# Ranking all eight experts by token count: the first two places are picked early, behind chunks 6 and 7

## The chip, the cores and the metric

One NeuronCore of a Trainium2 chip runs the whole program. The metric is the device time of one execution in microseconds (us), lower is better.

## What is computed

Three stages on 2304 tokens of width 512: local plus downsampled attention, a gated MLP, and a mixture of 8 experts with one expert per token. The last stage is the one the change works on:

```python
logits = xn @ en.T / tau
expert_idx = np.argmax(logits, axis=1)
...
for e in range(E):
    mask = expert_idx == e
    h = np.maximum(x[mask] @ w1[e], 0.0)
    out[mask] = gate_w[mask, None] * (h @ w2[e])
```

`w1[e]` is 512 x 1024 and `w2[e]` 1024 x 512, in f32. The inputs are fixed (seed 0). Counted with the reference, the experts get 297, 284, 329, 305, 296, 231, 280 and 282 tokens.

## The kernel before

**Work and order.** The tokens go through the gated MLP in 9 chunks of 256 (chunks 2 and 3, and 4 and 5, as pairs). Behind each chunk its rows are stored to `x2d` in DRAM, the router picks an expert per token, and `base`, a running count per expert (plus the start of that expert's part of the table), is raised. The tokens' entries (row, gate) go by an indirect DMA, a scatter, into two tables `tab` in DRAM. Then the experts run one after another in eight *places*. A place has a fixed number of columns (`CAPS`, line 50): token slots that are computed whether they are filled or not. Every product is made of three matmuls, with each operand split into a high and a low part.

**A place.** For a place the kernel reads its table rows (`tb`, line 1699 for places 0 and 1; 1760 and 1766 for the others), merges the two tables on DVE (line 1705), gathers the tokens' rows from `x2d` into `xs` (line 1720; in groups of 32 rows, line 1792, from place 2 on), transposes them on TensorE (line 1731), splits them, and runs layer 1 (line 1851, the place's columns as the moving operand) and layer 2 (line 1957 with the columns moving for places 1 to 6; line 1861 with 512 moving columns for places 0 and 7 and for the last 80 slots of place 0). That is 96 matmuls of line 1851 and 96 of line 1957 for a place from 1 to 6. Weights come in eight loads of 512 KB (lines 1663 and 1666, on the SP queue), each cast to a high part on ACT (line 1644) and subtracted on DVE (line 1647): a *split* is the pair.

**Which expert sits where.** Place 0 is always expert 0 (`FIXED = 1`), so its weights and its first 256 slots can be fetched while chunk 8 still runs. The other seven are ranked by count behind chunk 8 (`last_base`, line 1415): rank by comparing all pairs, then the inverse permutation into `ordi` (line 1435). SP and POOL load `ordi` into registers (line 1460), and every address of places 1 to 7 is computed from them. A queue that loads a register waits there for DVE's `ordi`; what stands behind it in that queue waits too. Place 1 has the same 336 columns as place 0, the others 312, 304, 288, 288, 288 and 256. If a count is over its place's columns, a block at the end (line 2168) computes the rest.

**What sets the order.** A planner written into the kernel (`Sched`) runs all steps as generators with planned durations, priorities and buffer slots, and so fixes in advance the order of instructions on each engine and queue; the hardware keeps that order and waits by semaphores. A weight load takes three slots of the pool `w`: one for the raw weights, two for the parts; slots come back from the gated MLP's weights as chunk 8 finishes with them. The DMA itself only waits for its raw slot.

Of the kernel before, what the change touches and what calls it, by code (L numbers as in the profile page):

```python
# [11 lines left out]
F32 = mybir.dt.float32  # L12
# [3 lines left out]
I32 = mybir.dt.int32  # L16
# [3 lines left out]
ALU = mybir.AluOpType  # L20
AX = mybir.AxisListType
# [3 lines left out]
P = 128  # L25
# [5 lines left out]
E = 8  # L31
# [8 lines left out]
NCHUNK = NTOK // CT  # L40
# [5 lines left out]
CAP = sum(SLT)  # L46
NSL = len(SLT)
EARLY = 256
FIXED = 1
CAPS = (CAP, CAP, 312, 304, 288, 288, 288, 256)  # L50
SLTE = [tuple(m for m in (P, P, n - 2 * P) if m) for n in CAPS]
NOV = -(-(NTOK - EARLY) // P)
EST = EARLY + NOV * P
FREE = float(np.uint32(0x3FFFFFFF).view(np.float32))
NEG = -1.0e30
NT18 = NTOK // P
NRK = E - FIXED
NCST = P + P // 2 + NPAIR * WK // 2 + 3 * E + 4 * NT18 + NOV + NRK
NEYE = P + P // 2
DMA_T = 700.0  # L60
# [233 lines left out]
def build(tc, a):  # L294
    nc = tc.nc
# [11 lines left out]
    out = a["out"]  # L307
# [3 lines left out]
    sc = Sched()  # L311
# [6 lines left out]
    def op(eng, ns, prio=None, how=None):  # L318
        return ("op", eng, ns, prio, how)
# [29 lines left out]
    o = 0  # L349
# [25 lines left out]
    rk = cst.tile([P, 4, NRK], F32, name="rk")  # L375
    rk2 = cst.tile([P, NRK, NRK], F32, name="rk2")
    ordi = cst.tile([P, NRK], I32, name="ordi")
    nc.gpsimd.memset(cape, float(CAP))


    slots("w", wp, NW, [P, 1024], True)
# [1033 lines left out]
    def last_base():  # L1415
        yield op("DVE", 75, -0.9, True)
        nc.vector.tensor_tensor(out=base, in0=base, in1=base0, op=ALU.subtract)
        r0, lo = iota8[:, 0, 0:NRK], iota8[:, 0, FIXED:]
        key, rank, val = rk[:, 0], rk[:, 1], rk[:, 2]
        inner = lambda x: x.unsqueeze(1).to_broadcast([P, NRK, NRK])  # L1420
        outer = lambda x: x.unsqueeze(2).to_broadcast([P, NRK, NRK])
        yield op("DVE", 75, -0.9, True)
        nc.vector.scalar_tensor_tensor(out=key, in0=lo, scalar=-1.0 / 16, in1=base[:, FIXED:], op0=ALU.mult, op1=ALU.add)
# [18 lines left out]
        nc.vector.tensor_reduce(out=cape[:, FIXED:], in_=rk2, axis=AX.X, op=ALU.add)  # L1442
# [11 lines left out]
    def set_order():  # L1454

        yield ("wait", "order")
        yield ("lag", 500)
        for i in range(NRK):
            on_ = [mybir.EngineType.SP] + ([mybir.EngineType.Pool] if FIXED + i == 1 else [])
            turn[FIXED + i] = nc.values_load(ordi[0:1, i:i + 1], engines=on_, min_val=FIXED, max_val=E - 1,  # L1460
                                             skip_runtime_bounds_check_because="a permutation of the ranked experts")
        sc.set("turns")

    def expert_of(x, e):

        return x[e] if e < FIXED else x[bass.ds(turn[e], 1)].rearrange("o r c -> (o r) c")

    def tab_rows(t, e, lo, hi):
        return expert_of(tabs[t].rearrange("(e s) w -> e s w", e=E)[:, lo:hi, :], e)
# [126 lines left out]
    def route_base(c, lp, rp):  # L1596
        for m in range(2):
            yield op("DVE", 80, -0.9)
            nc.vector.tensor_tensor(out=base, in0=base, in1=rp[:, 1, m, :], op=ALU.add)
        sc.put("ps", lp)  # L1600
        if c == NCHUNK - 2:

            yield op("DVE", 75, -0.9)
            nc.vector.tensor_scalar(out=base[:, 0:1], in0=base[:, 0:1], scalar1=float(EARLY), scalar2=None, op0=ALU.max)
        sc.set(("base", c))

    def store_x2(c, m, row):
        t = 2 * c + m
# [42 lines left out]
    def load_experts():  # L1651
        yield ("wait", ("g1", NCHUNK - 2))
        for e in range(E):
            if e == FIXED:
                yield ("wait", "turns")
            for nm, dst in (("w1", w1s), ("w2", w2s)):
                for i in range(4):
                    lo = yield ("get", "w")
                    hi = yield ("get", "w")
                    raw = yield ("get", "w")  # L1660
                    yield dma(P * 4096)
                    if nm == "w1":
# [11 lines left out]
    def load_slots(e, parts):  # L1674

        if e not in xss:
            xh = yield ("get", "xh")
            xl = yield ("get", "xl")
            tb = ep[0].tile([P, 2, NSL, 4], I32, tag=f"tb{e % 3}", name=f"tb{e}")
            xss[e] = (xh, xl, tb[:, 0])  # L1680
            tbs[e] = tb
        xh, xl = xss[e][0:2]
        tb = tbs[e]
        xhr, xlr = xh.bitcast(F32R), xl.bitcast(F32R)
        first = [j for j in parts if (e, j) in ((0, 2), (1, 0))]
        for j in first:
            sc.spawn(sc.cur.prio + 0.1 * j, load_slot(e, j, tb[:, 0], xhr, xlr))
        if (e, 2) == (0, parts[0]) or e == 1:
            for m in range(2):
                yield ("wait", ("tab", NCHUNK - 1) if m else "tab0")  # L1690
        soon = e == 0 or e == 1
        js = slice(parts[0], parts[-1] + 1)
        if e >= FIXED:
            yield ("wait", "turns")
        for t in range(2):
            yield op("POOL", 700, -1.0) if soon else dma(P * 48)
            if t == 0:
                sc.cur.t -= sc.LAT["POOL"] if soon else sc.LAT_DMA
            (nc.gpsimd if soon else nc.sync).dma_start(
                out=tb[:, t, js], in_=tab_rows(t, e, js.start * P, js.stop * P).rearrange("(j p) w -> p j w", p=P))  # L1700
        if soon:
            yield ("lag", 2900)
            yield tick()
        yield op("DVE", 80, -1.0, True)
        nc.vector.tensor_tensor(out=tb[:, 0, js], in0=tb[:, 0, js], in1=tb[:, 1, js], op=ALU.bitwise_and)
        tb = tb[:, 0]
        for j in parts:
            sc.set(("tb", e, j))
            if j not in first:
                sc.spawn(sc.cur.prio + 0.1 * j, load_slot(e, j, tb, xhr, xlr))  # L1710
# [424 lines left out]
    with tc.manual_schedule():  # L2135
# [93 lines left out]
def consts():  # L2229
# [8 lines left out]
    for n in range(NT18):  # L2238
# [3 lines left out]
    one = m.transpose(1, 2, 0, 3).reshape(64, NU * WK)  # L2242
    parts = [np.eye(P, dtype=np.float32), halves(np.eye(P, dtype=np.float32)), halves(m.reshape(P, -1)), np.tile(e, (P, 2)), np.tile(EST * e, (P, 1)),
             t.reshape(P, -1).view(np.float32), np.tile(EARLY + P * np.arange(NOV, dtype=np.float32), (P, 1)),
             np.tile(np.array(CAPS[FIXED:], np.float32), (P, 1))]
# [43 lines left out]
```

## Time and profile before

| | us |
|---|---|
| median of 3 runs (all three) | 811.74 (811.62, 811.74, 813.75) |
| the profiled execution, its own time | 808.81 |
| its span, first to last instruction | 807.2 |
| TensorE busy | 789.4 (98%), clock 0.997 of full speed |
| DVE, ACT, POOL busy | 563.2, 369.1, 195.1 |

Times in the trace count from the start of the span. Chunk 8's first matmul starts at 514.7, place 0's at 567.2, place 1's at 603.5, place 2's at 635.6, and the span ends at 807.2. Busy TensorE time overlaps (matmuls are pipelined), so how fast it goes is read from starts.

### The profile page before, as it was taken

The page shows a single profiled execution, that of the slowest core. Times are in us where ns is not written, and L with a number is a line of the kernel's source. Part 1 is how long each engine was busy: PE and PEld are TensorE (multiplying, and loading weights), DVE is VectorE, ACT ScalarE, POOL GpSimd, SP SyncE. Part 2 cuts the span into 40 slices and gives each one's busy share as a digit, 9 for nine tenths or more (in the row PEclk, how much of TensorE's full clock was granted, in tenths as well). Part 3 has the DMA queues.
Part 4 walks back from the last instruction along what each step waited for, and adds up shares of the span by engine and source line. Part 5 has one row for each costly group of instructions (what it writes and reads, how often), then busy time and mean ns, then how long its engine had stood idle before and what let it go on. Part 6 is the DMA issues. An engine that isn't in the chain of part 4 may idle for free. (4 is left out here: it accounts for less than half of the span.)

```text
span 807.2 us, 16215 instructions
## 1 busy us (share of the span) xinstructions
PE 789.4 (98%) x6122; PEld 691.1 (86%) x6128; DVE 563.2 (70%) x1472; ACT 369.1 (46%) x919; POOL 195.1 (24%) x208
## 2 busy tenths in 40 slices
PE   8989999999999999999999999999989999999997
PEld 5778778877877877877899999999979999999996
DVE  5899889768755468656399997675568778657620
ACT  3887788662332261232241312335345555545531
POOL 5533300010000010000013312012357163555201
PEclk9999999999999999999999999999999999999999
DMA  8995255512201112201143010052189666676401
GB/s 248 283 285 169 63 202 183 166 66 88 75 1 61 62 65 88 75 1 61 67 131 62 19 41 1 27 149 87 29 237 275 217 198 189 180 221 191 156 14 42
DMA packets 64371, 96.35 MB, mean 119 GB/s; under 512 B 15085, under 2 KB 34031, under 8 KB 64160
## 3 DMA queue, kind: packets, MB, share of 16 engines
q1 hardware_dynamic: 59424, 85.50, 34.9%
q0 software_dynamic: 4576, 9.51, 4.0%
q8 instruction: 49, 0.80, 0.4%
q14 instruction: 34, 0.28, 0.1%
q10 hardware_dynamic: 288, 0.26, 0.1%
HBM read 85.42 MB, written 10.29 MB: 119 GB/s over the span
## 5 line engine op out<-in xcount | busy, mean ns | idle before, releaser
L1176 PE MATMUL ps<-xb,w 128*128 128x512 f32 x512 | 171.9, 398 | 0.0
L1120 PE MATMUL ps<-xb,w 128*128 128x256 f32 x960 | 128.1, 285 | 0.3 <-ACT w L726 0.3
L1120 PEld LDWEIGHTS ps<-xb,w 128*128 128x128 f32 x960 | 121.8, 191 | 2.2 <-ACT w L726 0.5
L1176 PEld LDWEIGHTS ps<-xb,w 128*128 128x128 f32 x512 | 96.1, 188 | 22.4 <-issue 0.8
L1851 PE MATMUL ps<-xh,w 128*128 128x288 f32 (+4 forms) x512 | 111.2, 299 | 0.2
L1176 PE MATMUL ps<-xl,w 128*128 128x512 f32 x256 | 100.6, 393 | 0.0
L1851 PEld LDWEIGHTS ps<-xh,w 128*128 128x128 f32 x512 | 84.9, 188 | 1.2 <-ACT sg L1921 1.0
L1647 DVE TENSOR_TENSOR w<-w,w 128x1024 fp32r<-128x1024 f32 x64 | 76.6, 1217 | 8.2 <-ACT w L1644 7.5
L1851 PE MATMUL ps<-xl,w 128*128 128x288 f32 (+4 forms) x256 | 75.9, 296 | 0.0
L1792 POOL DMA_INDIRECT xs<-x2d,w x55 | 64.1, 1166 | 23.0 <-issue 14.3
L1644 ACT CAST w<-w 128x1024 fp32r<-128x1024 f32 x64 | 65.9, 1050 | 0.0
L1835 ACT ACTIVATE eh<-ps 128x288 fp32r<-128x288 f32 (+4 forms) x62 | 26.0, 419 | 83.9 <-PE ps L1851 73.7
L1837 DVE SCALAR_TENSOR_TENSOR el<-ps,eh 128x288 fp32r<-128x288 f32 (+4 forms) x62 | 28.0, 456 | 51.7 <-ACT eh L1835 51.2
L1176 PEld LDWEIGHTS ps<-xl,w 128*128 128x128 f32 x256 | 48.2, 188 | 8.7
L1238 PE MATMUL x<-w,hh 128*128 128x512 f32 x160 | 50.2, 395 | 0.0
L1851 PEld LDWEIGHTS ps<-xl,w 128*128 128x128 f32 x256 | 48.2, 188 | 0.2
L1957 PE MATMUL x<-eh,w 128*128 128x288 f32 (+3 forms) x192 | 46.8, 301 | 0.0
L1957 PE MATMUL ps<-eh,w 128*128 128x288 f32 (+3 forms) x192 | 46.8, 301 | 0.0
L1135 ACT ACTIVATE th<-ps 128x256 f32<-128x256 f32 x64 | 21.1, 380 | 50.8 <-PE ps L1176 50.8
L1150 ACT CAST hh<-th 128x256 fp32r<-128x256 f32 x64 | 24.1, 407 | 39.8 <-DVE th L1144 39.5
L1208 PE MATMUL x<-w,hh 128*128 128x512 f32 x128 | 41.2, 403 | 0.0
L1137 DVE SCALAR_TENSOR_TENSOR th<-th,ps 128x256 f32<-128x256 f32 x64 | 24.1, 415 | 24.5 <-ACT th L1135 24.3
(343 smaller groups left out, 1691.6 us busy)
## 6 DMA issues: line engine op xcount, KB each, us to landing
w<-w SPq DMA_DIRECT2D x64, 512.0 KB
w<-w_gate SPq DMA_DIRECT2D x10, 512.0 KB
w<-w_val SPq DMA_DIRECT2D x10, 512.0 KB
w<-w_out SPq DMA_DIRECT2D x10, 512.0 KB
aw<-qk SPq DMA_DIRECT2D x16, 291.0 KB
x2d<-sg SPq DMA_DIRECT2D x18, 256.0 KB
w<-qk SPq DMA_DIRECT2D x12, 291.0 KB
xl<-x2d SPq DMA_DIRECT2D x13, 256.0 KB
```

The costliest lines, as they stand in the source:

```text
L1120: nc.tensor.matmul(ps[:, o:o + CT], ww[:, k, fs], xx[:, k, :], start=(k == 0 and n == 0), stop=(k == KD - 1 and n == 2))
L1137: nc.vector.scalar_tensor_tensor(out=th, in0=th, scalar=1.0, in1=pg[:, r], op0=ALU.add, op1=ALU.mult)
L1176: nc.tensor.matmul(ps, ww[:, k, fs], xx[:, :, k], start=(k == 0 and n == 0), stop=(k == KD - 1 and n == 2))
L1208: nc.tensor.matmul(x2p[x], l, r[:, js], start=(u == 0 and n == 0), stop=(u == 2 * NFB - 1 and n == 2))
L1238: nc.tensor.matmul(x2p[c, m], l[:, j, ms], r[:, js], start=(p == 0 and j == 0 and n == 0), stop=(p == NFB - 1 and j == 1 and n == 2))
L1644: nc.scalar.copy(hi.bitcast(F32R), raw)
L1647: nc.vector.tensor_tensor(out=lo.bitcast(F32R), in0=raw, in1=hi.bitcast(F32R), op=ALU.subtract)
L1792: nc.gpsimd.indirect_dma_start(out=xs[:, n * P:(n + 1) * P], out_offset=None, in_=x2d.rearrange("t (a d) -> (t a) d", a=KD), in_offset=bas ...
L1835: nc.scalar.activation(hh[:, j, 0:n].bitcast(F32R), ps[:, 0:n], AF.Relu)
L1837: nc.vector.scalar_tensor_tensor(out=hl[:, j, 0:n].bitcast(F32R), in0=ps[:, 0:n], scalar=0.0, in1=hh[:, j, 0:n].bitcast(F32R), op0=ALU.max ...
L1851: nc.tensor.matmul(ps[:, 0:n], ww[:, k, fs], xx[:, k, 0:n], start=(k == 0 and t == 0), stop=(k == KD - 1 and t == 2))
L1957: nc.tensor.matmul(ys[d][:, 0:n], ww, h, start=(f == 0 and t == 0), stop=(f == NF2 - 1 and t == 2))
```

## The change

`FIXED` is gone. Behind chunk 6, DVE picks the expert with the highest count for place 0 (`pick(0)`), behind chunk 7 the highest of the others for place 1 (`pick(1)`); ties go to the lower number. Each goes as an integer (`onei`) into a register of SP and of POOL (`set_one`). The ranking behind chunk 8 adds 8192 and 4096 to the picked ones' keys, so that they come out as ranks 0 and 1, and `ordi` is loaded by SP alone, for places 2 to 7. Loads and tables of place 0 wait for the first pick, those of place 1 for the second, no longer for `ordi`. The columns become 336, 312, 312, 304, 288, 288, 288, 256. The first 256 slots of place 0 are kept free of chunk 8's tokens with `floor` instead of on expert 0.

```diff
-FIXED = 1
-CAPS = (CAP, CAP, 312, 304, 288, 288, 288, 256)
+CAPS = (CAP, 312, 312, 304, 288, 288, 288, 256)
...
-NRK = E - FIXED
+NRK = E
...
     def last_base():
...
+        nc.vector.scalar_tensor_tensor(out=key, in0=lo, scalar=-1.0 / 16, in1=base, op0=ALU.mult, op1=ALU.add)
+        yield op("DVE", 75, -0.9, True)
+        nc.vector.tensor_tensor(out=key, in0=key, in1=rk[:, 3], op=ALU.add)
...
     def set_order():
...
-        for i in range(NRK):
-            on_ = [mybir.EngineType.SP] + ([mybir.EngineType.Pool] if FIXED + i == 1 else [])
-            turn[FIXED + i] = nc.values_load(ordi[0:1, i:i + 1], engines=on_, min_val=FIXED, max_val=E - 1,
+        for i in range(2, E):
+            turn[i] = nc.values_load(ordi[0:1, i:i + 1], engines=[mybir.EngineType.SP], min_val=0, max_val=E - 1,
...
     def route_base(c, lp, rp):
...
         if c == NCHUNK - 2:
-            yield op("DVE", 75, -0.9)
-            nc.vector.tensor_scalar(out=base[:, 0:1], in0=base[:, 0:1], scalar1=float(EARLY), scalar2=None, op0=ALU.max)
+            yield ("wait", "picked")
+            yield op("DVE", 75, -0.9, True)
+            nc.vector.tensor_tensor(out=base, in0=base, in1=floor, op=ALU.max)
+        if c >= NCHUNK - 3:
+            sc.spawn(sc.cur.prio, pick(c - NCHUNK + 3))
...
+    def pick(i):
+        key, up_, got = rk[:, 0], rk[:, 2], rk[:, 3]
+        lo = iota8[:, 0, :]
+        nc.vector.tensor_tensor(out=key, in0=base, in1=base0, op=ALU.subtract)
+        nc.vector.scalar_tensor_tensor(out=key, in0=lo, scalar=-1.0 / 16, in1=key, op0=ALU.mult, op1=ALU.add)
+        if i == 1:
+            nc.vector.tensor_tensor(out=key, in0=key, in1=got, op=ALU.subtract)
+        nc.vector.tensor_reduce(out=one[:, i:i + 1], in_=key, axis=AX.X, op=ALU.max)
+        nc.vector.tensor_scalar(out=up_, in0=key, scalar1=one[:, i:i + 1], scalar2=None, op0=ALU.is_equal)
+        nc.vector.tensor_tensor(out=key, in0=up_, in1=lo, op=ALU.mult)
+        nc.vector.tensor_reduce(out=one[:, 2 + i:3 + i], in_=key, axis=AX.X, op=ALU.add)
+        nc.vector.tensor_copy(onei[:, i:i + 1], one[:, 2 + i:3 + i])
...
+    def set_one(i):
+        yield ("wait", ("one", i))
+        turn[i] = nc.values_load(onei[0:1, i:i + 1], engines=[mybir.EngineType.SP, mybir.EngineType.Pool], min_val=0, max_val=E - 1,
...
     def load_experts():
...
-            if e == FIXED:
-                yield ("wait", "turns")
+            yield ("wait", ("turn", e) if e < 2 else "turns")
...
     def load_slots(e, parts):
...
-        if e >= FIXED:
-            yield ("wait", "turns")
+        yield ("wait", ("turn", e) if e < 2 else "turns")
```

(The `yield op(...)` lines of `pick`, which only tell the planner a duration, are left out, and the last two operations of each pick, which set `floor` and `got`.)

The change moves instructions at three places. The order of TensorE's instructions stays; only their columns change.

**POOL behind chunk 8.** `tab_86` and `tab_87` are the two tables, `tb_5715` and `tb_5732` place 0's copy of its table rows, `tb_5830` and `tb_5858` place 1's. Before:

```order
L1387 DMA tab_86<-cn,si_5998 18432x4
L1387 DMA tab_87<-cn,si_5998 18432x4
L1699 DMA tb_5715<-tab_86 128x4
L1460 TENSOR_LOAD ordi
L1699 DMA tb_5715<-tab_87 128x4
L1699 ISA
L1699 DMA tb_5830<-tab_86 128x3x4
```

With the change (line numbers are those of the changed file):

```order
L1388 DMA tab_86<-cn,si_6040 18432x4
L1388 DMA tab_87<-cn,si_6040 18432x4
L1742 ISA
L1742 DMA tb_5732<-tab_86 128x4
L1742 ISA
L1742 DMA tb_5732<-tab_87 128x4
L1742 ISA
L1742 DMA tb_5858<-tab_86 128x3x4
```

The load of `ordi` is gone from POOL; two loads of `onei` stand further up, one behind chunk 6's scatters and one behind chunk 7's.

**DVE behind chunk 8**, from the ranking to place 0's merged table. The lines 128x1024 are splits, `el` place 0's second layer's low parts. Before:

```order
L1647 TENSOR_TENSOR w_5_5796<-w_4_5814,w_5_5797 128x1024
L1427 TENSOR_REDUCE rk<-rk_92 128x7
L1647 TENSOR_TENSOR w_4_5823<-w_5_5859,w_4_5846 128x1024
L1429 TENSOR_TENSOR rk_92<-rk,cn 128x49
L1431 TENSOR_TENSOR rk_92<-rk_92,cn 128x49
L1433 TENSOR_REDUCE rk<-rk_92 128x7
L1435 CAST ordi<-rk 128x7
```

With the change:

```order
L1692 TENSOR_TENSOR w_4_5851<-w_5_5887,w_4_5874 128x1024
L1430 TENSOR_REDUCE rk<-rk_92 128x8
L1692 TENSOR_TENSOR w_6_5913<-w_5_5915,w_5_5914 128x1024
L1432 TENSOR_TENSOR rk_92<-rk,cn 128x64
L1692 TENSOR_TENSOR w_5_5922<-w_4_5935,w_5_5928 128x1024
L1434 TENSOR_TENSOR rk_92<-rk_92,cn 128x64
L1880 SCALAR_TENSOR_TENSOR el_1_5624<-ps_1_115,eh_1_5622 128x256
L1436 TENSOR_REDUCE rk<-rk_92 128x8
L1880 SCALAR_TENSOR_TENSOR el_1_5624<-ps_1_114,eh_1_5622 128x256
L1438 CAST ordi<-rk 128x8
L1692 TENSOR_TENSOR w_4_5942<-w_6_6011,w_5_6010 128x1024
L1441 TENSOR_TENSOR rk_92<-rk,cn 128x64
```

Splits of place 1's `w1` (the third, fifth and eleventh row) now stand among the ranking; before they stood behind both merges. Between line 1417 (now 1418) and place 0's merge (line 1705, now 1748) there were two splits and twelve small operations of the ranking and the overflow count; now there are five splits and nine small ones, and a sixth split stands between that merge and place 1's.

**SP around the stores of chunk 8's rows.** `w_4_6198` holds place 2's table rows. Before:

```order
L1610 DMA x2d<-sg_1_107 128x512
L1610 DMA x2d<-sg_1_106 128x512
L1460 TENSOR_LOAD ordi x7
L1760 ISA
L1760 DMA w_4_6198<-tab_86 32x11x4
```

The first load of place 1's weights comes behind four such table reads.

With the change:

```order
L1655 DMA x2d<-sg_1_109 128x512
L1707 ISA
L1707 DMA w_7_6055<-w 128x4x256
L1655 DMA x2d<-sg_1_108 128x512
L1710 ISA
L1710 DMA w_3_6142<-w 128x2x512
L1710 ISA
L1710 DMA w_6_6206<-w 128x2x512
L1462 TENSOR_LOAD ordi x6
```

Ahead of these rows stand three more `w1` loads of place 1, so four `w1` loads and two of its four `w2` loads are issued before `ordi`; before it was none. One `w1` load stands between the two stores. The third `w2` load follows behind place 2's tables, the fourth later.

## Rows read from the trace of the kernel before

**Rows 1.** Waits of TensorE in the whole span: us in total, times, longest.

```profile
PE ps L1731 <- DMA xs<-x2d,tb: 2.9, 2, 1.7
```

**Rows 2.** Timeline of TensorE at the gathered rows' transposes: start, duration, instruction, wait before.

```profile
589.05 0.59 PE L1731 MATMUL ps<-eye,xs 80*128 80x80 f32 x4
...
592.79 0.74 PE L1731 MATMUL ps<-eye,xs 128*128 128x128 f32 x4 [1.71 <-DMA xs<-x2d,tb]
...
595.44 0.75 PE L1731 MATMUL ps<-eye,xs 128*128 128x128 f32 x4 [1.20 <-DMA xs<-x2d,tb]
```

**Rows 3.** The same timeline: starts around 24 matmuls of 336 and of 312 columns.

```profile
620.78 0.32 PE L1851 MATMUL ps<-xh,w 128*128 128x336 f32 x1
...
624.50 0.32 PE L1957 MATMUL x<-eh,w 128*128 128x336 f32 x1
...
651.24 0.30 PE L1851 MATMUL ps<-xh,w 128*128 128x312 f32 x1
...
654.66 0.31 PE L1957 MATMUL x<-eh,w 128*128 128x312 f32 x1
```

**Rows 4.** Busy time by stretch: PE, PEld, DVE, ACT, POOL, clock, DMA share, GB/s.

```profile
561.00:564.00 3.00, 3.00 (x17) 2.55 (x16) 1.27 (x3) 1.73 (x3) 0.00 (x0) 1.00 0.00 0
593.00:595.00 2.00, 1.24 (x7) 0.76 (x6) 1.17 (x2) 1.42 (x2) 0.53 (x1) 1.00 1.07 385
603.40:632.00 28.60, 28.60 (x179) 26.64 (x178) 21.94 (x42) 15.00 (x23) 19.98 (x17) 1.00 0.88 268
660.00:688.00 28.00, 28.00 (x205) 27.99 (x204) 21.33 (x34) 15.29 (x24) 11.77 (x9) 1.00 0.64 186
```

**Rows 5.** Timeline of POOL behind the last chunk's scatters.

```profile
574.67 1.79 POOL L1387 DMA_INDIRECT tab<-cn,si  x1 [0.48 <-DVE base L1378]
...
581.19 0.57 POOL L1699 DMA_DIRECT2D tb<-tab  x1 [4.12 <-DVE cape L1442]
...
584.20 1.05 POOL L1720 DMA_INDIRECT xs<-x2d,tb  x1 [0.30 <-issue]
586.30 1.03 POOL L1720 DMA_INDIRECT xs<-x2d,tb  x1 [1.05 <-DVE w L1771]
587.64 1.00 POOL L1720 DMA_INDIRECT xs<-x2d,tb  x1 [0.30 <-issue]
```

**Rows 6.** Landing of the scatters L1387, and POOL's load of `ordi`, L1460.

```profile
DMA to landing us min/median/max: 3.0/3.0/3.0
...
L1460 POOLq TENSOR_LOAD <-ordi x1: 498/498/498, 580.1 to 580.1; - x1
```

**Rows 7.** Landing times: the gathers L1720 after 580, then the group gathers L1792.

```profile
DMA to landing us min/median/max: 6.4/7.1/7.8
...
DMA to landing us min/median/max: 2.5/3.7/7.4
```

**Rows 8.** Timeline of DVE: base after chunk 7; then a split, the ranking, the merges.

```profile
534.65 0.15 DVE L1604 TENSOR_SCALAR base<-base 128x1 f32<-128x1 f32 x1
...
575.58 0.42 DVE L1837 SCALAR_TENSOR_TENSOR el<-ps,eh 128x256 fp32r<-128x256 f32 x1
...
576.81 1.22 DVE L1647 TENSOR_TENSOR w<-w,w 128x1024 fp32r<-128x1024 f32 x1
577.95 0.20 DVE L1427 TENSOR_REDUCE rk<-rk 128x7 f32<-128x49 f32 x1
...
583.18 0.16 DVE L1705 TENSOR_TENSOR tb<-tb 128x4 int32<-128x4 int32 x1 [0.80 <-DMA tb<-tab]
585.36 0.17 DVE L1705 TENSOR_TENSOR tb<-tb 128x12 int32<-128x12 int32 x1 [2.02 <-DMA tb<-tab]
```

**Rows 9.** Timeline of the SP queue: loads of w2 (place 0), stores of x2d, loads of w1.

```profile
539.15 10.65 SPq L1666 DMA_DIRECT2D w<-w  x4
566.29 1.70 SPq L1610 DMA_DIRECT2D x2d<-sg  x2
...
585.09 2.99 SPq L1663 DMA_DIRECT2D w<-w  x4
```

More of the change, by code (lines that the diff above doesn't have):

```diff
@@ L377, in build @@
     ordi = cst.tile([P, NRK], I32, name="ordi")
-    nc.gpsimd.memset(cape, float(CAP))
+    one = cst.tile([P, 4], F32, name="one")
+    onei = cst.tile([P, 2], I32, name="onei")
+    floor = cst.tile([P, E], F32, name="floor")
     slots("w", wp, NW, [P, 1024], True)
@@ L1417, in last_base @@
         nc.vector.tensor_tensor(out=base, in0=base, in1=base0, op=ALU.subtract)
-        r0, lo = iota8[:, 0, 0:NRK], iota8[:, 0, FIXED:]
+        r0 = lo = iota8[:, 0, :]
         key, rank, val = rk[:, 0], rk[:, 1], rk[:, 2]
@@ L1422, in last_base @@
         yield op("DVE", 75, -0.9, True)
-        nc.vector.scalar_tensor_tensor(out=key, in0=lo, scalar=-1.0 / 16, in1=base[:, FIXED:], op0=ALU.mult, op1=ALU.add)
+        nc.vector.scalar_tensor_tensor(out=key, in0=lo, scalar=-1.0 / 16, in1=base, op0=ALU.mult, op1=ALU.add)
+        yield op("DVE", 75, -0.9, True)
+        nc.vector.tensor_tensor(out=key, in0=key, in1=rk[:, 3], op=ALU.add)
         yield op("DVE", 110, -0.9, True)
@@ L1441, in last_base @@
         yield op("DVE", 100, -0.8)
-        nc.vector.tensor_reduce(out=cape[:, FIXED:], in_=rk2, axis=AX.X, op=ALU.add)
+        nc.vector.tensor_reduce(out=cape, in_=rk2, axis=AX.X, op=ALU.add)
         yield op("DVE", 75, -0.8, True)
@@ L1457, in set_order @@
         yield ("lag", 500)
-        for i in range(NRK):
-            on_ = [mybir.EngineType.SP] + ([mybir.EngineType.Pool] if FIXED + i == 1 else [])
-            turn[FIXED + i] = nc.values_load(ordi[0:1, i:i + 1], engines=on_, min_val=FIXED, max_val=E - 1,
-                                             skip_runtime_bounds_check_because="a permutation of the ranked experts")
+        for i in range(2, E):
+            turn[i] = nc.values_load(ordi[0:1, i:i + 1], engines=[mybir.EngineType.SP], min_val=0, max_val=E - 1,
+                                     skip_runtime_bounds_check_because="a permutation of the ranked experts")
         sc.set("turns")
     def expert_of(x, e):
-        return x[e] if e < FIXED else x[bass.ds(turn[e], 1)].rearrange("o r c -> (o r) c")
+        return x[bass.ds(turn[e], 1)].rearrange("o r c -> (o r) c")
     def tab_rows(t, e, lo, hi):
@@ L1601, in route_base @@
         if c == NCHUNK - 2:
-            yield op("DVE", 75, -0.9)
-            nc.vector.tensor_scalar(out=base[:, 0:1], in0=base[:, 0:1], scalar1=float(EARLY), scalar2=None, op0=ALU.max)
-        sc.set(("base", c))
+            yield ("wait", "picked")
[3 more added lines that the diff above has]
+            sc.spawn(sc.cur.prio, pick(c - NCHUNK + 3))
+        sc.set(("base", c))
+    def pick(i):
+        key, up_, got = rk[:, 0], rk[:, 2], rk[:, 3]
+        lo = iota8[:, 0, :]
+        yield op("DVE", 75, -0.7, True)
+        nc.vector.tensor_tensor(out=key, in0=base, in1=base0, op=ALU.subtract)
+        yield op("DVE", 75, -0.7, True)
+        nc.vector.scalar_tensor_tensor(out=key, in0=lo, scalar=-1.0 / 16, in1=key, op0=ALU.mult, op1=ALU.add)
+        if i == 1:
+            yield op("DVE", 75, -0.7, True)
+            nc.vector.tensor_tensor(out=key, in0=key, in1=got, op=ALU.subtract)
+        yield op("DVE", 80, -0.7)
+        nc.vector.tensor_reduce(out=one[:, i:i + 1], in_=key, axis=AX.X, op=ALU.max)
+        yield op("DVE", 75, -0.7, True)
+        nc.vector.tensor_scalar(out=up_, in0=key, scalar1=one[:, i:i + 1], scalar2=None, op0=ALU.is_equal)
+        yield op("DVE", 75, -0.7, True)
+        nc.vector.tensor_tensor(out=key, in0=up_, in1=lo, op=ALU.mult)
+        yield op("DVE", 80, -0.7)
+        nc.vector.tensor_reduce(out=one[:, 2 + i:3 + i], in_=key, axis=AX.X, op=ALU.add)
+        yield op("DVE", 75, -0.7, True)
+        nc.vector.tensor_copy(onei[:, i:i + 1], one[:, 2 + i:3 + i])
+        sc.set(("one", i))
+        if i == 0:
+            yield op("DVE", 75, -0.7, True)
+            nc.vector.scalar_tensor_tensor(out=floor, in0=up_, scalar=float(EARLY), in1=base0, op0=ALU.mult, op1=ALU.add)
+            yield op("DVE", 75, -0.7, True)
+            nc.vector.tensor_scalar(out=got, in0=up_, scalar1=8192.0, scalar2=None, op0=ALU.mult)
+            sc.set("picked")
+        else:
+            yield op("DVE", 75, -0.7, True)
+            nc.vector.scalar_tensor_tensor(out=got, in0=up_, scalar=4096.0, in1=got, op0=ALU.mult, op1=ALU.add)
@@ L1607, in store_x2 @@
+    def set_one(i):
+        yield ("wait", ("one", i))
+        yield ("lag", 500)
+        turn[i] = nc.values_load(onei[0:1, i:i + 1], engines=[mybir.EngineType.SP, mybir.EngineType.Pool], min_val=0, max_val=E - 1,
+                                 skip_runtime_bounds_check_because="the place of a maximum among the experts")
+        sc.set(("turn", i))
     def store_x2(c, m, row):
@@ L2150, in build @@
         sc.spawn(NCHUNK * 10 + 3, turn_slots(), 0.0)
+        for i in range(2):
+            sc.spawn(NCHUNK * 10 + 3, set_one(i), 0.0)
         sc.spawn(NCHUNK * 10 + 3, set_order(), 0.0)
@@ L2244, in consts @@
              t.reshape(P, -1).view(np.float32), np.tile(EARLY + P * np.arange(NOV, dtype=np.float32), (P, 1)),
-             np.tile(np.array(CAPS[FIXED:], np.float32), (P, 1))]
+             np.tile(np.array(CAPS, np.float32), (P, 1))]
     return {"cst": np.concatenate(parts, axis=1), "tri": np.triu(np.ones((P, P), np.float32), 1),
```

## The prediction

> **What bounds the kernel now.** TensorE does: it is busy for 789.4 of 807.2 us at full clock (the table above). So the first view to read is what TensorE itself waits for. One line of that list lies in the stretch that the change touches [rows 1]: 2.9 us before the transposes of line 1731, for gathered rows. The timeline shows where: place 0's last 80 rows are transposed at 589.05 without a wait, then place 1's first two tiles are waited for, 1.71 us before 592.79 and 1.20 us before 595.44 [rows 2]. Apart from those two holes TensorE goes through from place 0 to place 6, and there only the number of columns counts.
>
> Why are place 1's rows late? Follow their chain backwards. The two gathers are issued on POOL at 586.30 and 587.64 [rows 5], so they land after 6.5 us (592.8) and 7.8 us (595.4); the landing line says the same, 6.4 to 7.8 [rows 7]. Ahead of them stand the table merges on DVE, at 583.18 and 585.36, both waiting for the table reads [rows 8]. The reads stand on POOL behind the load of `ordi`: the second scatter is issued at 574.67 and lands after 3.0 us, at 577.7, yet the next table read starts only at 581.19, after `ordi` was loaded at 580.1 plus 0.5 [rows 5, 6]. So place 1 pays twice: its tables wait for the ranking, and its gathers then share the DMA engines with its own weights, whose four `w1` loads go out at 585.09 [rows 9]; at 593 to 595 the DMA share is 1.07, while it was 0.00 at 561 to 564 [rows 4].
>
> **Term 1: 24 columns fewer at place 1.** The 192 matmuls of place 1 (96 of line 1851, 96 of line 1957) have 312 columns for 336. 24 of them at 336 take 624.50 - 620.78 = 3.72 us, and 24 at 312, place 2's, 654.66 - 651.24 = 3.42 us [rows 3]. That is 0.30 us per 24, and 8 x 0.30 = **2.4 us**, all on the path. The last tile (56 rows for 80) makes the transposes and drains a little shorter; I count nothing.
>
> One thing could speak against this term. In place 2 and 3 the weight loads of TensorE (PEld) are busy 27.99 of 28.00 us, at place 1 26.64 of 28.60 [rows 4]: they have less and less room as columns fall. But the rows of 312 columns are measured inside such a stretch, so the 3.42 us already holds whatever the weight loads cost. The Trainium skill ("Perfetto Trace Analysis", Identifying the Most-Contended Engine) says that TensorE's headroom is to be judged by LDWEIGHTS busy share and not by matmul busy time; taken literally, place 1 could give back only its 7%, 2.0 us, and the sum would be 0.4 us smaller. The trace decides for 2.4.
>
> **Term 2: the two waits.** The gathers' issue moves little. On POOL `ordi` is gone, so the table reads can start when the scatters have landed, at about 577.8, some 3 us earlier. But the merges on DVE now stand behind five splits. From 575.58 on, five splits at 1.14 (577.95 - 576.81), four `el` operations at up to 0.42 and nine small ones at 0.1 to 0.2 [rows 8] make 8 to 9 us: the first merge comes at 583.6 to 584.8 (before 583.18), the second one split later at 585.0 to 586.2 (before 585.36). So what POOL wins DVE takes back, and place 1's first gather goes out at 585.9 to 587.1 instead of 586.30, I take 586.3.
>
> The landing is what changes. Four `w1` and two `w2` loads of place 1 are now issued before `ordi`, most of them in the stretch where the DMA engines idle [rows 4], and the stores of chunk 8's rows (566.29 before, [rows 9]) stay ahead of the gathers by 15 us. The four 512 KB loads that went out from 585.09 on [rows 9] are gone from there; one `w2` load, which now follows place 2's tables, is left beside the gathers. How fast a 256 KB gather lands then, no row shows. From above it is bounded by 6.4 to 7.8 us [rows 7]; from below by the quarter-size group gathers, 2.5 us at best and 3.7 in the middle [rows 7]; the nearest row is place 0's last tile, 160 KB, issued at 584.20 and used without a wait at 589.05, so within 4.85 us though the weights came on top of it [rows 2, 5]. I take 5.5. (The Trainium skill, "DMA: Bandwidth & Descriptors", Anatomy of one DMA, has a fit of 2.0 us plus bytes over 436 GB/s for a DMA of GpSimd; 256 KB would be 2.6 us, an estimate from that page which no run here shows, and with it both waits would vanish.)
>
> With 5.5, the first tile lands at 591.8; TensorE wants it at 592.79 - 1.71 = 591.08, so 0.7 us of the 1.71 stay. The second, issued 1.34 us later, lands at 593.1; TensorE wants it 1.45 us after it took the first (595.44 - 1.20 - 592.79), at 593.2: no wait. 2.2 us are saved. From this goes what place 0's last tile may lose: its gather is issued about 0.7 us later than before, and it had at least no wait at 589.05; I take 0.1. Term 2 is **2.1 us**. Ends: at 4.7 us or less both waits vanish (2.9); at 6.4 and 7.8 with DVE at its late end nothing is saved and place 0's tile adds 0.7 (-0.7).
>
> **What costs nothing, and its cover.** The two picks are some ten DVE operations of 0.15 to 0.2 us each [rows 8], 2 to 3 us in a stage where DVE is busy 1.27 of 3.00 us [rows 4]. Pick 1 ends about 3 us behind 534.65 [rows 8], at 538; on POOL place 0's table reads stand behind it, but chunk 7's scatters, issued behind the same counts, land 3.0 us later anyway [rows 6]. On SP the `w2` loads of place 0 stand behind it, and they went out at 539.15 [rows 9]. If pick 1 came 2 us late, it would be covered still: place 0's second layer needs those weights after 575. Pick 0 is a whole chunk earlier. `ordi` comes some 2.5 us later for the same splits; only place 2's tables wait for it, and its products start at 635.6. The ranking over 8 instead of 7 adds 1 operation. With the counts given above no place overflows: expert 2 (260 behind chunk 6, 329 in the end) gets 336 columns, expert 4 (273 behind chunk 7, 296) gets 312, and 305, 297, 284, 282, 280, 231 fit into 312, 304, 288, 288, 288, 256.
>
> **Sum.** 2.4 + 2.1 = 4.5 us. The profiled execution of 808.81 us becomes 804.3. It lies 2.9 us under the median of the runs, 811.74, against which I predict **807.2 us** (-0.55%). By the ends: 2.4 + 2.9 = 5.3 and 2.4 - 0.7 = 1.7, so 806.4 to 810.0.
>
> **Rivals.**
> 1. *The waits stay.* The gathers' landing is not set by the weights, or DVE is so late that the earlier bytes do not help. For it: DVE's queue grows by three splits, and the gathers on POOL are issued no earlier. Against it: a DMA share of 1.07 in just the holes. Then only term 1 is left: 811.74 - 2.4 = 809.3, at the edge of no change. Chance 0.14, with partial savings under 0.3 us in it.
> 2. *Slower: an early split holds its queue.* On ACT the casts of place 1's `w1` now stand between place 0's activations, on DVE its splits ahead of the merges. Each waits for its load; if the fourth `w1` load, issued behind the first store at 566 to 567, were not in by about 578, when its cast's turn comes, all behind it on ACT and then TensorE would stop. For it: place 1's gathers took up to 7.8 us at a full DMA. Against it: the engines are nearly empty then. It decides against the change from where TensorE loses over 4.5 us; with a load in at 585, 7 us late, the time is 811.74 - 4.5 + 7 = 814.2. Chance 0.04.
> 3. *The change does not do what it says:* a count over its place's columns sends an expert into the block at the end, which loads 4 MB; at the 268 GB/s of the busiest place [rows 4] that alone is 16 us, so 823 us or more. The counts speak against it: 0.01.
>
> **How the numbers follow.** My forecast has 0.81. A measurement of this kernel tells 0.3% (2.4 us) from no change. Faster by more than that are the forecast and its inner ends from a saving of 2.5 us on: 0.81. Within 0.3% is rival 1 with the low end of term 2: 0.14. Slower: rivals 2 and 3, 0.05. The range goes from 806.4 less 0.8, since the three runs differ by up to 2.1 us, to the upper end 810.0 with 0.4 for the same reason: 805.6 to 810.4. That covers rival 1 and leaves rivals 2 and 3 out.
>
> **What would show it.** In the changed profile 24 matmuls of place 1 take 3.42 us; the list of TensorE's waits has 0 to 1 us at the transposes in place of 2.9; place 1's gathers are issued at about 586 and land in 5 to 6 us; the DMA share at 593 to 595 is well under 1. Term 2 is wrong if gathers issued at the same time still land in 6.4 us or more, or if they are issued over 1 us later than before. The whole is wrong if TensorE waits for `eh` or `el` in place 0.

## The result, and the profile after

The median of the changed kernel is **805.7 us** (four runs, 805.35 to 806.44), beside four runs of the kernel before at 811.62 to 814.24, median 812.75: ratio 0.9913, 95% interval 0.9892 to 0.9935. On another chip it had 804.71 us against 810.62, ratio 0.992 [0.9895, 0.9946], and a copy of it (below) 5.6 us less than before. So the gain is 5.6 to 7.0 us by the medians; the forecast was 4.5, and 807.2 us, with a range from 805.6 on, so that 805.7 lies just inside its low end.

The profiled execution after has 805.35 us, its span is 803.7. That is 3.5 us less than the profiled span before, but the spans can't be compared as they stand: the stores of chunk 7's rows to `x2d`, which the change does not touch, went out from 511.85 us on, before from 514.14. From here on times are also given from the start of these stores ("the 514 store"). By them the end moved from 293.06 to 291.85 us only. The stores before, and in a second profile of the changed kernel that is used below:

```profile
514.14 1.68 SPq L1610 DMA_DIRECT2D x2d<-sg  x2
```

```profile
514.23 1.68 SPq L1655 DMA_DIRECT2D x2d<-sg  x2
```

The list of TensorE's waits from 560 us on (us in total, times, longest), where [rows 1] had one line of 2.9:

```profile
PE ps L1774 <- DMA xs<-x2d,tb: 1.5, 2, 0.9
PE ps L1894 <- issue: 0.8, 1, 0.8
PE ps L2000 <- issue: 0.4, 1, 0.4
PE x L2000 <- issue: 0.3, 1, 0.3
```

Half of the wait is still there, and three holes without a releaser are new. TensorE's timeline (start, duration, instruction, wait before), for [rows 2] and [rows 3]:

```profile
586.76 0.59 PE L1774 MATMUL ps<-eye,xs 80*128 80x80 f32 x4
...
589.67 0.75 PE L1774 MATMUL ps<-eye,xs 128*128 128x128 f32 x4 [0.89 <-DMA xs<-x2d,tb]
...
591.69 0.75 PE L1774 MATMUL ps<-eye,xs 128*128 128x128 f32 x4 [0.57 <-DMA xs<-x2d,tb]
...
610.45 0.30 PE L2000 MATMUL x<-eh,w 128*128 128x312 f32 x1 [0.28 <-issue]
611.16 0.40 PE L2000 MATMUL ps<-eh,w 128*128 128x312 f32 x1 [0.41 <-issue]
...
621.05 0.31 PE L2000 MATMUL x<-eh,w 128*128 128x312 f32 x1
...
624.47 0.30 PE L1894 MATMUL ps<-xh,w 128*128 128x312 f32 x1
```

The last two rows are 24 matmuls of place 1: 624.47 - 621.05 = 3.42 us, as forecast. POOL's gathers (the first is place 0's last tile) and, of DVE, the merges with the splits about them, for [rows 5] and [rows 8]:

```profile
581.80 1.78 POOL L1763 DMA_INDIRECT xs<-x2d,tb  x1 [3.09 <-DVE tb L1748]
583.89 1.76 POOL L1763 DMA_INDIRECT xs<-x2d,tb  x1 [0.30 <-DVE cn L1447]
585.95 1.00 POOL L1763 DMA_INDIRECT xs<-x2d,tb  x1 [0.30 <-DMA xs<-x2d,tb]
```

```profile
580.09 1.22 DVE L1692 TENSOR_TENSOR w<-w,w 128x1024 fp32r<-128x1024 f32 x1
...
581.36 0.15 DVE L1748 TENSOR_TENSOR tb<-tb 128x4 int32<-128x4 int32 x1
581.43 1.22 DVE L1692 TENSOR_TENSOR w<-w,w 128x1024 fp32r<-128x1024 f32 x1
...
582.70 0.17 DVE L1748 TENSOR_TENSOR tb<-tb 128x12 int32<-128x12 int32 x1
...
583.52 1.21 DVE L1692 TENSOR_TENSOR w<-w,w 128x1024 fp32r<-128x1024 f32 x1
```

With the 2.29 us of the early start put back, place 1's gathers are issued at 586.18 and 588.24 (forecast 586.3 and 587.64). The first is used at 589.67, so it landed after 5.8 us. The DMA engines are still full at 587 to 589, with the gathers, one w2 load and place 2's tables, and nearly empty soon after, where before they were at 1.07 from 593 to 595 [rows 4] (busy time by stretch, columns as there):

```profile
587.00:589.00 2.00, 1.79 (x9) 1.18 (x8) 1.22 (x4) 1.37 (x2) 0.69 (x1) 1.00 1.13 342
590.00:592.00 2.00, 1.43 (x9) 0.96 (x8) 1.40 (x2) 0.59 (x1) 0.64 (x1) 1.00 0.21 52
593.00:595.00 2.00, 2.00 (x16) 1.83 (x15) 1.18 (x2) 1.44 (x3) 1.39 (x3) 1.00 0.12 33
```

### The profile page after: what moved, and what is told of

It is laid out like the page before. It is cut to its first block, busy times and chain, and to the rows that moved or that the text cites. A ratio compares the mean times of both kernels' runs of the same rounds, so it can differ in the third digit from the quotient of the medians.

```text
span 803.7 us, 16258 instructions
## 1 busy us (share of the span) xinstructions
PE 787.3 (98%) x6122; PEld 689.2 (86%) x6128; DVE 567.9 (71%) x1493; ACT 367.1 (46%) x917; POOL 198.3 (25%) x207
## 5 line engine op out<-in xcount | busy, mean ns | idle before, releaser
L1894 PE MATMUL ps<-xh,w 128*128 128x288 f32 (+3 forms) x512 | 110.3, 297 | 1.0 <-issue 0.8
L1894 PE MATMUL ps<-xl,w 128*128 128x288 f32 (+3 forms) x256 | 75.5, 295 | 0.0
L1835 POOL DMA_INDIRECT xs<-x2d,w x55 | 67.4, 1226 | 27.0 <-issue 14.6
L1880 DVE SCALAR_TENSOR_TENSOR el<-ps,eh 128x288 fp32r<-128x288 f32 (+3 forms) x62 | 27.9, 453 | 54.2 <-ACT eh L1878 44.8
L1878 ACT ACTIVATE eh<-ps 128x288 fp32r<-128x288 f32 (+3 forms) x62 | 25.8, 416 | 80.1 <-PE ps L1894 65.7
L2000 PE MATMUL ps<-eh,w 128*128 128x288 f32 (+2 forms) x192 | 46.4, 300 | 0.4 <-issue 0.4
L2000 PE MATMUL x<-eh,w 128*128 128x288 f32 (+2 forms) x192 | 46.4, 299 | 0.3 <-issue 0.3
```

Of the source, the lines that this page charges most:

```text
L1835: nc.gpsimd.indirect_dma_start(out=xs[:, n * P:(n + 1) * P], out_offset=None, in_=x2d.rearrange("t (a d) -> (t a) d", a=KD), in_offset=bas ...
L1878: nc.scalar.activation(hh[:, j, 0:n].bitcast(F32R), ps[:, 0:n], AF.Relu)
L1880: nc.vector.scalar_tensor_tensor(out=hl[:, j, 0:n].bitcast(F32R), in0=ps[:, 0:n], scalar=0.0, in1=hh[:, j, 0:n].bitcast(F32R), op0=ALU.max ...
L1894: nc.tensor.matmul(ps[:, 0:n], ww[:, k, fs], xx[:, k, 0:n], start=(k == 0 and t == 0), stop=(k == KD - 1 and t == 2))
L2000: nc.tensor.matmul(ys[d][:, 0:n], ww, h, start=(f == 0 and t == 0), stop=(f == NF2 - 1 and t == 2))
```

## The experiments

Of each profiled execution, in us: the waits ahead of place 1's first and second tile, the start of its first product and the end of the span, both counted from the 514 store, and the stretch between 590 and 606 us in which the granted clock was below full speed. "Filled" and the other names are explained below.

| kernel | waits | first product | end | clock below 1.00 |
|---|---|---|---|---|
| before, first profile | 1.71, 1.20 | 89.33 | 293.06 | nowhere |
| before, second | 2.72, 0 | 90.53 | 294.36 | 593 to 598 |
| before, third | 1.58, 1.22 | 91.79 | 295.57 | 592 to 600 |
| before, longer rows | 1.96, 0.92 | 91.85 | 295.56 | 594 to 602 |
| before, filled | 1.06, 0 | 89.45 | 293.16 | nowhere |
| before, filled, second | 0.50, 0.43 | 89.30 | 293.09 | nowhere |
| changed, first profile | 0.89, 0.57 | 88.16 | 291.85 | nowhere |
| changed, second | 0.98, 0.54 | 88.24 | 289.67 | nowhere |
| changed, longer rows | 1.03, 0 | 87.72 | 289.18 | nowhere |
| changed, 336 columns | 0.96, 0 | 87.47 | 291.01 | nowhere |
| changed, late weights | 0, 0 | 88.12 | 289.54 | nowhere |
| changed, merges first | 0, 0 | 87.25 | 288.81 | nowhere |
| changed, merges and memset first | 0, 0 | 86.15 | 287.61 | nowhere |
| the same, second | 0, 0 | 86.15 | 287.66 | nowhere |

**Where do 2.3 us at the start come from?** The change makes a row of the constants `cst` 1,120 instead of 1,116 bytes long. Two kernels add one unused column:

```
-NCST = ... + NOV + NRK
+NCST = ... + NOV + NRK + 1
```

> The kernel before with one unused zero column at the end of the constants `cst`: its rows become 280 columns (1,120 bytes), as in the changed kernel, instead of 279 (1,116 bytes); the order of instructions is that of before. Theory: the changed kernel is 2.3 us ahead already at 170 us, far ahead of anything the change touches, because the first loads read `cst` by rows of another length. Then this kernel is 2.3 us faster than before (ratio 0.997), and its stores of chunk rows to `x2d` come at about 169.5, 289.0 and 564.0 us instead of 171.95, 291.36 and 566.29. Rival: the 2.3 us are the scatter of single executions; then this kernel equals before (ratio within 0.999 to 1.001) and its stores come at any of these times.

Measured: 811.11 us against 810.47, ratio 1.0012 [0.9992, 1.0031]; the 514 store at 514.14, as in the first profile of before.

> The changed kernel with one unused zero column more in `cst`: 281 columns, 1,124 bytes a row. Theory (row length matters): it loses 2.3 us against the changed kernel, about 808 us, ratio to before 0.994. Rival (scatter): it equals the changed kernel, about 805.7 us, ratio 0.991.

Measured: 804.89 us, ratio 0.9939 [0.9922, 0.9956]; the 514 store at 512.02. Row length plays no part. Over all profiles that store comes between 511.85 and 515.09 us with either program; the 2.3 us are scatter of single executions. This copy of the changed kernel also had none of the holes at 610 and 691 us. But the copy of the kernel before showed something else, a stretch at half clock behind the two waits, to which the runs below come back.

**What are 24 columns worth?**

```
-CAPS = (CAP, 312, 312, 304, 288, 288, 288, 256)
+CAPS = (CAP, CAP, 312, 304, 288, 288, 288, 256)
```

> The changed kernel with 336 instead of 312 columns for place 1: the early picks, the early tables and weights stay, the saved columns go. The forecast's term 1 says that this is 2.4 us slower than the changed kernel: about 808.1 us where that has 805.7, ratio to before 0.994. Rival: the two holes of about 1 us each that the changed kernel's TensorE shows at 610 and 691 us, with no releaser, belong to the columns (weight loads or evictions that no longer keep up at 312), and 312 columns give back only about 1.2 us; then this kernel takes about 806.9 us (ratio 0.9925) and has no such holes.

Measured: 806.7 us, ratio 0.9957 [0.9942, 0.9971], 1.8 us more than the copy above. In the traces, from place 1's first product to place 3's, it takes 61.27 us, before 61.48, the changed kernel's second profile 59.25. The two products in the first profile of before, then in that second profile:

```profile
603.47 0.32 PE L1851 MATMUL ps<-xh,w 128*128 128x336 f32 x1
...
664.95 0.30 PE L1851 MATMUL ps<-xh,w 128*128 128x304 f32 x1
```

```profile
602.47 0.31 PE L1894 MATMUL ps<-xh,w 128*128 128x312 f32 x1
...
661.72 0.30 PE L1894 MATMUL ps<-xh,w 128*128 128x304 f32 x1
```

So the columns give 2.0 to 2.2 us there, and the early pick alone 3.8 us by the median. (The shorter last tile takes 0.3 us of the columns' gain back, ahead of this stretch; see the part on the prediction.)

**What is left of the waits?** The merges stand behind splits on DVE. Two kernels change the order of instructions only:

```
         nc.scalar.copy(hi.bitcast(F32R), raw)
+        if key[0:2] == ("w1", 1):
+            yield ("wait", ("tb", 1, 0))
         yield from stand_back()
```

> The changed kernel with the splits of place 1's w1 on VectorE held back behind place 1's table merges (order only). Theory: the rest of 1.5 us of waits at place 1's transposes is there because the merges stand behind splits (581.36 and 582.70 us) though the tables have landed. Then the merges come at about 579.8 us, the gathers at 580.2, 582.2 and 584.2 us, 1.6 us earlier, land after 5.7 us as before, and TensorE no longer waits there: 1.4 us faster than the changed kernel, about 804.3 us, ratio to before 0.9895. Rival: the tables land no earlier than the merges ran, or the splits, now late, hold place 1's first products at 600 us: 805.7 us or more.

Measured: 803.22 us, ratio 0.9915 [0.9895, 0.9935]. Both waits are gone; a wait of 1.02 us at place 1's third tile is new. DVE's memset of that tile's buffer and two splits, then POOL's gather of the tile:

```profile
589.96 0.48 DVE L1761 MEMSET xs<- 56x512 f32 x1 [0.62 <-PE ps L1776]
590.37 1.15 DVE L1694 TENSOR_TENSOR w<-w,w 128x1024 fp32r<-128x1024 f32 x1
...
591.84 1.21 DVE L1694 TENSOR_TENSOR w<-w,w 128x1024 fp32r<-128x1024 f32 x1
```

```profile
590.75 3.18 POOL L1765 DMA_INDIRECT xs<-x2d,tb  x1 [3.56 <-DVE xs L1761]
```

The expectation of the next run says that the memset stood behind splits. The rows don't show that: it waited 0.62 us for TensorE (the transposes of place 0's last tile), and the gather goes out 76.46 us behind the 514 store, as in the changed kernel (76.46 and 76.47). What is new is that it holds POOL for 3.18 us instead of 1.00, beside two splits. The next kernel puts the other splits of place 1 behind that gather:

```
+        if key[1] == 1:
+            yield ("wait", ("tb", 1, 0) if key[0] == "w1" and key[2] < 2 else ("gather", 1, 2))
```

> The changed kernel with place 1's splits on VectorE held back further than in the run before it: the first two of w1 behind the table merges, the other two and w2's behind the third gather of place 1 (order only), because the memset ahead of that gather stood behind splits and TensorE waited 1.02 us for its rows. Theory: no wait at any of place 1's transposes, 1.0 us less than with the merges alone: about 802.2 us where that had 803.2, ratio 0.990. Rival: the splits, now up to 6 us later, hold place 1's first products at 600 us, or the next weights come late; then it is no faster than 803.2 us, with a wait for w at place 1's first products.

Measured: 803.15 us, ratio 0.9907 [0.9888, 0.9927]. The third gather now takes 2.05 us, beside one split, and no wait is left. Repeated beside the changed kernel:

> The version with the merges and the memset ahead of place 1's splits once more, beside the changed kernel on the same chip. Theory: it is 1.5 us faster than the changed kernel (the 1.5 us of waits that that has left), ratio to before 0.990 to 0.991 where the changed kernel has 0.993. Rival: the two are equal, since what the waits give is lost elsewhere.

Measured: 803.17 us, ratio 0.9905 [0.9876, 0.9934], the changed kernel 804.71. From the 514 store it ends 2.0 us earlier than that (287.66 against 289.67). Its transposes, no wait among them:

```profile
588.85 0.59 PE L1776 MATMUL ps<-eye,xs 80*128 80x80 f32 x4
590.71 0.63 PE L1776 MATMUL ps<-eye,xs 128*128 128x128 f32 x4
591.88 0.63 PE L1776 MATMUL ps<-eye,xs 128*128 128x128 f32 x4
595.58 0.68 PE L1776 MATMUL ps<-eye,xs 56*128 56x56 f32 x4
```

By the medians it is 1.5 us under the changed kernel, though the two sets of six runs overlap (800.84 to 805.74 us and 802.71 to 805.57); by the traces 2.0 us, and the copy with longer rows (289.18) still 1.5.

**Do early weights matter?**

```
-            yield ("wait", ("turn", e) if e < 2 else "turns")
+            yield ("wait", ("turn", e) if e < 1 else "turns")
```

(in `load_experts` alone.)

> The changed kernel with the weight loads of place 1 waiting for the ranking again, as in before; its early pick, its tables and the 312 columns stay. Theory (the weights' transfers set the landing): place 1's gathers have four 512 KB loads beside them again and land after 6.4 to 7.8 us instead of 5.7; since VectorE has no early splits, the merges and the gathers come some 2 us earlier than in the changed kernel, so that the waits come out at 1 to 2 us in sum and the time at 805 to 807 us. Rival: a gather of 256 KB lands in 5.7 us whatever runs beside it; then the gathers, 2 us earlier, arrive in time, TensorE doesn't wait there, and the time is about 1.5 us under the changed kernel's: 804.2 us.

Measured: 804.95 us, ratio 0.9936 [0.9918, 0.9954]: the same as with early weights (804.89 in the copy above and 804.71 below, on other chips). POOL's gathers of place 0's last and place 1's three tiles, then TensorE's transposes of these four:

```profile
582.43 1.05 POOL L1763 DMA_INDIRECT xs<-x2d,tb  x1 [0.88 <-DVE tb L1748]
583.97 1.04 POOL L1763 DMA_INDIRECT xs<-x2d,tb  x1 [0.49 <-DVE xs L1759]
585.31 1.00 POOL L1763 DMA_INDIRECT xs<-x2d,tb  x1 [0.30 <-issue]
590.23 1.00 POOL L1763 DMA_INDIRECT xs<-x2d,tb  x1 [3.92 <-DVE xs L1759]
```

```profile
588.68 0.59 PE L1774 MATMUL ps<-eye,xs 80*128 80x80 f32 x4
590.54 0.63 PE L1774 MATMUL ps<-eye,xs 128*128 128x128 f32 x4
591.96 0.75 PE L1774 MATMUL ps<-eye,xs 128*128 128x128 f32 x4
597.35 0.69 PE L1774 MATMUL ps<-eye,xs 56*128 56x56 f32 x4 [1.51 <-DMA xs<-x2d,tb]
```

Without early splits the first gather goes out 70.21 us behind the 514 store (583.97 - 513.76), with them 72.04, and TensorE waits for neither of the first two tiles. The trace has the landing of the first: 4.5 us. It went out 0.5 us ahead of the four `w1` loads (584.46), where before it came 1.2 us behind them (586.30 and 585.09) and took 6.5. The third, 56 rows or 112 KB, went out among the loads, with the DMA engines' share at 1.05 to 1.24 from 589 to 597; it took 7.1 us and cost 1.51. With the merges and the memset first, the first gather goes out as early (70.40 and 70.02 us) with early weights; there the third tile is not waited for, and the end comes 1.9 us sooner (287.61 and 287.66 against 289.54). So the early weights spare the third tile a wait of 1.5 us, and in the changed kernel their splits cost the first two as much.

**And the clock?**

> The kernel before, unchanged, for a second profile of it. Theory (clock): its profiled execution shown at first (808.81 us) had TensorE at full clock behind the two waits, but the copy of it with longer rows of constants had the granted clock at 0.50 from about 594.5 to 601 us, directly behind waits of 1.96 and 0.92 us, and reached place 1's first product 2.5 us later for it; executions of before scatter between these two cases. A second profile shows the one or the other: place 1's first product 89.3 us behind the store of 514 us (full clock) or 91.8 us (clock down). Rival: the fall at 594 us was a single event and has nothing to do with the waits; then nothing like it is seen again in any profile of before.

> The kernel before, unchanged, for a third profile. Theory (clock): behind waits of 2.7 to 2.9 us in sum the granted clock is 0.50 for some us between 593 and 602 us, as in the second profile of before and in the copy with longer rows, and place 1's first product comes 1.2 to 2.5 us later than the 89.3 us behind the store of 514 us that the first profile has. Rival: at full clock as in the first profile; then the fall is no more than every second execution's.

Both profiles of before have the fall. Busy time by stretch of the third profile (PE, PEld, DVE, ACT, POOL, clock, DMA share, GB/s):

```profile
590.00:592.00 2.00, 1.44 (x7) 0.97 (x7) 0.52 (x2) 0.66 (x2) 0.00 (x0) 1.00 1.04 357
592.00:594.00 2.00, 0.78 (x5) 0.77 (x5) 0.65 (x1) 0.87 (x1) 1.46 (x2) 0.56 1.09 347
594.00:596.00 2.00, 2.00 (x7) 1.61 (x6) 1.47 (x2) 0.91 (x2) 0.55 (x1) 0.50 1.16 230
596.00:598.00 2.00, 2.00 (x10) 1.73 (x9) 0.69 (x2) 1.41 (x3) 1.05 (x2) 0.50 0.32 50
598.00:600.00 2.00, 2.00 (x15) 2.00 (x15) 1.23 (x1) 1.52 (x2) 1.70 (x2) 0.74 0.45 164
600.00:602.00 2.00, 2.00 (x20) 2.00 (x19) 1.64 (x3) 1.83 (x3) 1.70 (x2) 1.00 0.80 222
```

Here TensorE waits twice, the clock goes to 0.50, which is 1.2 GHz, and 7 matmuls start from 594 to 596 where the first profile of before, at full clock, has 13 from 596 to 598, behind its own second wait. In the three executions with the fall (the last is the copy with longer rows) the first product comes 1.20, 2.46 and 2.52 us later than there. Is it the waits that do it? The next kernel leaves the rows as late and keeps TensorE busy with products whose result is overwritten:

```
+            if e == 1 and j < 2 and k == 0:
+                for i in range(8 if j == 0 else 4):
+                    nc.tensor.matmul(ps[:, 0:3 * P], identb, eye.bitcast(BF16), start=True, stop=True)
             nc.tensor.transpose(ps[:, k * m:(k + 1) * m], quarter(xs, k)[:m], ident[:m, :m])
```

> The kernel before with the two holes filled: ahead of place 1's first transposes 8, ahead of its second 4 products of 128x384 in bf16 of constants, into the same ps tile that the transposes overwrite; the rows arrive no earlier. Theory (clock): TensorE waits as long for the rows, but is busy meanwhile, its clock stays at 1.00 from 590 to 606 us, and the time is that of the best executions of before, 808.7 us or 0.998 of its median, with the slow tail (over 811 us) gone. Rival: the clock plays no part; then the filler costs nothing and gains nothing, ratio 1.000, with the same scatter.

Measured: 809.16 us against 810.41, ratio 0.9989 [0.9972, 1.0005]. The clock stays up though the rows come no earlier:

```profile
592.00:594.00 2.00, 0.94 (x7) 0.78 (x7) 0.00 (x0) 0.04 (x1) 0.00 (x0) 1.00 1.08 383
594.00:596.00 2.00, 2.00 (x12) 1.24 (x11) 1.17 (x2) 1.49 (x2) 1.01 (x1) 1.00 1.08 330
596.00:598.00 2.00, 2.00 (x14) 1.69 (x13) 1.81 (x3) 1.82 (x3) 1.27 (x2) 1.00 0.94 202
```

> The kernel before with the two holes filled by constant products once more, for its time (the first try gave a ratio of 0.9989 with an interval that holds 1). Theory: three of four profiled executions of before lose 1.2 to 2.5 us to the clock behind the waits, 1.5 us in the mean, and the filler keeps the clock up: ratio 0.998, the granted clock of the single runs at 0.996 or 0.997 as in the first try, while those of before lie at 0.989 to 0.994; in the profile no clock fall between 590 and 606 us. Rival: the fall costs the kernel nothing on the whole; ratio 1.000 and granted clocks as before's.

Measured: 809.83 us against 810.03, ratio 1.0002 [0.9987, 1.0018]; the clock again at 1.00 from 590 to 606. Of the 24 filled runs 16 have a mean granted clock of 0.996 or 0.997, of the 61 runs of before on these chips two. But the time hardly follows: the mean of the 24 is 809.7 us, that of the 61 is 810.3; on one chip the filled runs are 1.1 us under the others in the mean, on the other 0.2.

> The changed kernel, unchanged, on the chip of the variants, with a second profile. Theory: of the 7.0 us that its median won at first, some 3.9 are there at full clock (2.2 from 24 columns, 1.6 from the waits) and the rest is that TensorE's clock no longer falls behind the waits, as it did in two of four profiled executions of before and its copy (1.2 and 2.5 us). Then the ratio is again 0.991 to 0.994, the clock stays at 1.00 from 590 to 606 us, and the two holes without a releaser at 610 and 691 us (2.1 us in sum) are not seen again, since they belonged to that one execution. Rival: the holes come back at the same places; then they belong to the changed program, and it could be 2 us faster without them.

Measured: 804.71 us, ratio 0.992 [0.9895, 0.9946]. Clock at 1.00 there, waits of 0.98 and 0.54, and the holes at 610 and 691 us are gone, as in every variant. With them the first profile ends 2.2 us later from the 514 store (291.85 against 289.67); they belonged to that execution, and what made them is open.

## Why the prediction was right, and by how much it was not

**Term 1, 2.4 us.** Right, and 0.2 us too large. 24 matmuls take 3.42 us, and from place 1 to place 3 the second profile takes 61.48 - 59.25 = 2.2 us less; with 336 columns put back 2.0 us return.

**Term 2, 2.1 us.** The mechanism was right and the size too large. The waits went from 2.91 to 1.52 us (0.98 + 0.54; in the copies of the changed kernel 1.03 and 0.96), and place 1's first product came 1.1 us earlier (89.33 to 88.24). The step that failed is "the second, issued 1.34 us later, lands at 593.1 [...]: no wait". It was issued 2.06 us later, since the gather ahead of it held POOL for 1.76 us instead of 1.03. The splits that the change moves there cost DVE's queue what was forecast, and beyond it each gather that began beside a running split. The first tile's landing was sized at 5.5 us and was 5.8 to 5.9, where before's order has 6.3 to 7.3 for the same tile in six profiles.

A second step was mis-sized: "The last tile (56 rows for 80) makes the transposes and drains a little shorter; I count nothing." It cost 0.3 us. From the second tile's transposes to the first product it is 8.32 us in all three profiles with 56 rows and the changed order, 8.03 before, and 8.02 with 336 columns, which have 80 rows again. The third tile's four transposes and the matmul behind them, in the first profile of before and in the second of the changed kernel:

```profile
599.18 0.61 PE L1731 MATMUL ps<-eye,xs 80*128 80x80 f32 x4
599.59 0.44 PE L2065 MATMUL ps<-w,xh 128*80 128x256 f32 x2
```

```profile
597.96 0.68 PE L1774 MATMUL ps<-eye,xs 56*128 56x56 f32 x4
598.57 0.46 PE L2108 MATMUL ps<-w,xh 128*80 128x256 f32 x2
```

From start to start that is 0.41 us for 80 rows and 0.61 for 56, most of the 0.3; why the smaller tile takes longer no run shows. So of the 1.4 us that the waits lost, 1.1 are left at the first product.

**The sum.** At full clock the two profiles give 293.06 - 289.67 = 3.4 us instead of 4.5: 2.2 from the columns and 1.1 from the start of place 1. The time gained 5.6 to 7.0. So the number came out close by two misses that partly cancel, and the second is the step "it lies 2.9 us under the median of the runs, [...] against which I predict": that distance was taken as a constant which the change leaves alone. The profile that carried the forecast was a fortunate one. In three other profiled executions of this order the waits cost more than themselves, 1.2 to 2.5 us of half clock behind them, and in none of the changed kernel or its variants. The four profiles of before's order end 294.64 us behind the 514 store in the mean, 1.6 us later than the first; the changed kernel's second profile and its copy end at 289.67 and 289.18, 5.2 us sooner, near the 5.6 and 5.9 of the medians on those chips. But what this is worth in the median is not settled: filling the waits brought the clock back, but only 0.6 us of time in the mean, and its two intervals hold 1. Of the 2 us and more between the full-clock traces and the medians, some may be the clock, some scatter (the interval of the copy, 0.9922 to 0.9956, reaches down to 3.6 us); the runs don't divide them.

**The rivals.** The first (the waits stay) was half right: 1.5 of 2.9 us stayed, and the late weights show that the reason named for it, DVE's longer queue, is real. The second (an early split or cast holds its queue until TensorE stops) did not come: no line of the waits above names `eh`, `el` or `w` in place 0. The third (a count over its columns) did not come either.

## What to carry to other kernels

A wait of TensorE can cost more than its own length, since the work behind it may run at the lower clock: look at the granted clock behind each wait in more than one profiled execution before taking a profile's distance to the median as a constant. Work that is moved forward to be out of the way of one queue stands in another: here the splits of the early weights cost the first two gathers what the early weights spared the third, and by the traces an order with the small operations first gave 1.5 to 2.0 us more.

## What the runs showed of the hardware

A gather on POOL that begins while a split (a tensor_tensor of two SBUF operands, 1.2 us) is running on DVE ends 0.87 to 0.94 us behind the split, in fourteen gathers of the changed kernel and its variants. In the changed kernel's rows above the split that began at 583.52 ends at 584.73, and the gather that began at 583.89 ends at 585.65, 0.92 us behind it; the one at 581.80 ends 0.93 us behind the split of 581.43. One with two splits beside it, 3.18 us long, is shown above. A gather without a split beside it takes 0.97 to 1.06 us. Where the gather began first, it took 1.0 us all the same (599.23 in the kernel before, with a split from 599.28). The Trainium skill ("SBUF — State Buffer", Who interferes with whom) says that a DVE instruction with two SBUF inputs contends with a GpSimd instruction that reads SBUF, and that the order of issue decides which of the two is blocked; the trace agrees, 1.76 and 1.78 us for 1.00, though the same section reports a probe in which `tensor_tensor` did not stall a DMA.
